# Loading heads in sets of four of one side, through GpSimd's queue, with direct moves on SyncE's

## The chip, the cores and the metric

One core of one Trainium2 chip. The time is device microseconds of one launch; a comparison goes by the median of several runs. The kernel is written by hand in a language in which the order of the instructions of each engine is the order in which the program records them, and in which every engine works through its own queue in order: TensorE (PE), VectorE (DVE), ScalarE (ACT), GpSimd (POOL) and SyncE (SP), which only issues DMAs.

## The reference

Batch 4, 8 heads, 768 tokens, 64 dimensions of a head; all tensors are fp32.

```python
q_bits = (einsum('bhsd,dk->bhsk', q, proj) > 0)      # 6 bits, the same for k
mask   = q_bucket[..., :, None] == k_bucket[..., None, :]
scores = where(mask, q @ k.T / 8, -1e9)
attn   = softmax(scores) ;  attn_out = attn @ v
x      = attn_out as (4*768 tokens, 8*64)
h      = maximum(x @ w1, x @ w2, x @ w3)             # 512 -> 768
out    = h @ w_out                                   # 768 -> 512
```

A query sees only the keys whose six signs of a projection are its own.

## The kernel before, in words

**S, the operand of the scores.** For every head the scores need q and k with the head dimension on the partitions, and below it rows of +0.5 or -0.5, the hash bits (six, padded to eight). So one matmul over 64 + 8 = 72 rows gives the dot product and, added to it, a number that is largest where all bits agree; one exp with a bias then gives nearly zero for every other key. The tile S holds 72 rows, four slots of 768 columns in bf16. Before, a tile S belongs to a *pair*: two q heads and the same two k heads of one batch.

**How a pair is prepared**, in this order: `load` (L97) brings the pair's k and q into `nat` from HBM, two DMAs of 384 KB on SyncE. `turn` (L133) transposes 32 x 32 blocks on VectorE, four instructions T<-nat of 128 x 384, written at a step of four elements. `narrow` (L137) scales T to bf16 on GpSimd. `place` (L142, L147) writes that to DRAM (`td`) and reads it back in another order into rows 0 to 63 of S: three DMAs on SyncE. `hashes` (L153, L157, L160) projects T by fp32 matmuls (bp), VectorE takes the signs (`bits`), a DMA writes them to DRAM (`bd`); two units later `place_bits` (L164) reads them into rows 64 to 71 of S, again on SyncE. The scores of the pair wait for all of this. Pair 0 alone takes a shorter way: TensorE transposes it (L291), ACT and VectorE write S from PSUM.

**Units and groups.** A unit is one head, one half of the queries (384) and two blocks of 128 keys: two score matmuls (L179) and one exp on ACT (L181). Six units are a group (two heads, half the queries), eight groups a batch; there are 192 units. The order is batch, half, pair, so the first four groups touch all four pairs of batch 0. After a group come the `values` (av, L192) and `sums` (sm, L206) matmuls of its units, in a burst: every two units for units under 24, then every six, from unit 48 on every twelve. `normalize` gathers the sums by a DMA (dd, L233), inverts them on VectorE, spreads them over the partitions by way of DRAM (rd, rb, L240, L244) and scales the values into xT (L249), steps that are due 0, 5, 7, 11 and 12 units after the burst.

**FFN.** The tokens of one half of one batch make one FFN: 18 groups of four matmuls (L265) whose maximum VectorE keeps (ht, L269 and L271), then three output blocks (L278, copied by ACT in L281, sent by SyncE). These are put between units by a credit: each unit earns 0.68, a first-layer group costs 0.66, an output block 1.32. The first FFN starts at unit 37.

**What sets the order.** The main loop goes unit by unit: scores of the next unit, then whatever was put down for this unit by `when(u, ...)` or is due in `steps`, then FFN groups, then a burst. All DMAs but the weights' and the projection's go through SyncE's queue in this order, and a DMA there that waits for its data holds up those behind it. Weights come through GpSimd's queue at units 10 to 24. PSUM has two tiles for scores, one for av and three ("ms") for everything else.

Of the kernel before, what the change touches and what calls it, by code (L numbers as in the profile page):

```python
# [9 lines left out]
FP32 = mybir.dt.float32  # L10
# [7 lines left out]
def kernel(  # L18
# [30 lines left out]
    NU_G = NM  # L49
# [12 lines left out]
    nat_pool = ctx.enter_context(tc.tile_pool(name="nat", bufs=3))  # L62
    t32_pool = ctx.enter_context(tc.tile_pool(name="t32", bufs=2))
    t16_pool = ctx.enter_context(tc.tile_pool(name="t16", bufs=2))
    s_pool = ctx.enter_context(tc.tile_pool(name="spool", bufs=7))
    b_pool = ctx.enter_context(tc.tile_pool(name="bpool", bufs=2))
    vn_pool = ctx.enter_context(tc.tile_pool(name="vnpool", bufs=3))
    vo_pool = ctx.enter_context(tc.tile_pool(name="vopool", bufs=7))
# [5 lines left out]
    h_pool = ctx.enter_context(tc.tile_pool(name="hpool", bufs=10))  # L74
# [8 lines left out]
    pst = konst.tile([P, 2, NBITS], FP32, name="pst")  # L83
    ones = konst.tile([P, Q], FP16, name="ones")
    at_tiles = [konst.tile([P, 2, HALF + 2], FP16, name=f"AT{i}", tag=f"AT{i}") for i in range(NAT)]
# [3 lines left out]
    nat, t32, t16, s_of, vnat, vo = {}, {}, {}, {}, {}, {}  # L89

    def load(pi):
        b, jj = divmod(pi, HPAIR)
        nat[pi] = nat_pool.tile([P, NC * D], FP32, tag="nat", name="nat")
        for side, src in ((1, k), (0, q)):
            nc.sync.dma_start(nat[pi][side * D : (side + 1) * D, :],  # L97
                              src[b, 2 * jj : 2 * jj + 2].rearrange("h (t c) d -> (h t) (c d)", c=NC))

    def load_by_m(pi, m0, m1):  # L100
        b, jj = divmod(pi, HPAIR)
        if pi not in nat:
            nat[pi] = nat_pool.tile([P, NC * D], FP32, tag="nat", name="nat")
        n4 = nat[pi].rearrange("p (cc m d) -> p cc m d", cc=CC, d=D)
        for side, src, eng in ((1, k, nc.sync), (0, q, nc.scalar)):
            s4 = src[b, 2 * jj : 2 * jj + 2].rearrange("h (t cc m) d -> (h t) cc m d", cc=CC, m=NM)
            eng.dma_start(n4[side * D : (side + 1) * D, :, m0:m1, :], s4[:, :, m0:m1, :])

    def load_v(pi):
        b, jj = divmod(pi, HPAIR)  # L110
        vnat[pi] = vn_pool.tile([P, 2, NM * D], FP32, tag="vnat", name="vnat")
        nc.sync.dma_start(vnat[pi][:], v[b, 2 * jj : 2 * jj + 2].rearrange("h (p m) d -> p h (m d)", p=P))

    def cast_v(pi):
        vo[pi] = vo_pool.tile([P, 2, NM * D], FP16, tag="vo", name="vo")
        nc.gpsimd.tensor_copy(vo[pi][:], vnat.pop(pi)[:])  # L116
# [11 lines left out]
    def turn(pi, u, m0, m1):  # L128
        if pi not in t32:
            t32[pi] = t32_pool.tile([P, 2, S], FP32, tag="T32", name="T32")  # L130
        i_ = nat[pi].rearrange("p (cc m u d) -> p u m cc d", cc=CC, u=2, d=Q)[:, u, m0:m1]
        o = t32[pi].rearrange("p u (m t cc) -> p u m cc t", t=Q, cc=CC)[:, u, m0:m1]
        nc.vector.transpose(o, i_)  # L133

    def narrow(pi):
        t16[pi] = t16_pool.tile([P, 2, S], BF16, tag="T16", name="T16")
        nc.gpsimd.tensor_scalar(out=t16[pi][:], in0=t32[pi][:], scalar1=RS, scalar2=1.0,  # L137
                                op0=AluOp.mult, op1=AluOp.mult)

    def place(pi):  # L140
        td = drp.tile([P, 2, S], BF16, tag="td", name="td")
        nc.sync.dma_start(td[:], t16.pop(pi)[:])  # L142
        s = s_pool.tile([KR, 4, S], BF16, tag="S", name="S")
        s_of[pi] = s
        tv = td.rearrange("(x d) u n -> u d x n", d=Q)
        for u in range(2):
            nc.sync.dma_start(s[u * Q : (u + 1) * Q, :, :], tv[u])  # L147

    def hashes(pi):
        bp = ms_ps.tile([P, 512], FP32, tag="ms", name="bp")  # L150
        for u in range(2):
            for j in range(NJ):
                nc.tensor.matmul(bp[Q * j : Q * (j + 1), 0:JW], pj[:, u, :], t32[pi][:, u, j * JW : (j + 1) * JW],  # L153
                                 start=(u == 0), stop=(u == 1))
        del t32[pi]
        bits = b_pool.tile([P, JW], BF16, tag="bits", name="bits")
        nc.vector.tensor_scalar(out=bits[:], in0=bp[:, 0:JW], scalar1=0.0, scalar2=0.5,  # L157
                                op0=AluOp.is_gt, op1=AluOp.subtract)
        bd = drp.tile([KB, 4 * S], BF16, tag="bd", name="bd")
        nc.sync.dma_start(bd.rearrange("b (x j n) -> j (b x) n", x=4, j=NJ), bits[:])  # L160
        return bd

    def place_bits(pi, bd):
        nc.sync.dma_start(s_of[pi][D:KR].rearrange("b x n -> b (x n)"), bd[:])  # L164


    units = [(b, qh, jj, kp, hd) for b in range(B) for qh in range(2) for jj in range(HPAIR)
             for kp in range(MH) for hd in range(2)]
    NU = len(units)
    UPB = NU // B  # L170
    xts, avs_of, ys_of, sm_of, av_of = {}, {}, {}, {}, {}

    def scores(u):
        b, qh, jj, kp, hd = units[u]
        s = s_of[b * HPAIR + jj]
        sc = sc_ps.tile([P, 2, 512], FP32, tag="sc", name="sc")
        for j in range(2):
            m = 2 * kp + j
            nc.tensor.matmul(sc[:, j, 0:HALF], s[0:KR, 2 + hd, m * P : (m + 1) * P],  # L179
                             s[0:KR, hd, qh * HALF : (qh + 1) * HALF], start=True, stop=True)  # L180
        nc.scalar.activation(at_tiles[u % NAT][:, :, 0:HALF], sc[:, :, 0:HALF], ActFn.Exp, bias=EXP_BIAS, scale=SCALE)  # L181

    def values(g, kps):
        b, qh, jj = units[g * NU_G][0:3]
        if kps[0] == 0:
            av_of[g] = av_ps.tile([P, 512], FP32, tag="av", name="av")
        for kp in kps:
            for j in range(2):
                m = 2 * kp + j
                for hd in range(2):  # L190
                    at = at_tiles[(g * NU_G + 2 * kp + hd) % NAT]
                    nc.tensor.matmul(av_of[g][hd * D : (hd + 1) * D, 0 : HALF + 1],  # L192
                                     vo[b * HPAIR + jj][:, hd, m * D : (m + 1) * D], at[:, j, 0 : HALF + 1],
                                     start=(m == 0), stop=(m == NM - 1))

    def sums(g, kps):
        if kps[0] == 0 and g % 2 == 0:
            sm_of[g // 2] = ms_ps.tile([P, 512], FP32, tag="ms", name="sm")
        sm = sm_of[g // 2]
        for kp in kps:  # L200
            for j in range(2):
                m = 2 * kp + j
                for hd in range(2):
                    r = 2 * hd + g % 2
                    at = at_tiles[(g * NU_G + 2 * kp + hd) % NAT]
# [3 lines left out]
    def take_av(g):  # L209
        avs_of[g] = avs_pool.tile([P, HALF + 4], FP32, tag="avs", name="avs")  # L210
        nc.vector.tensor_copy(avs_of[g][:, 0 : HALF + 1], av_of.pop(g)[:, 0 : HALF + 1])  # L211

    def take_sums(gp):
        ys_of[gp] = ys_pool.tile([P, HALF], FP32, tag="ys", name="ys")
        nc.vector.tensor_copy(ys_of[gp][:], sm_of.pop(gp)[:, 0:HALF])


    def normalize(gp):
        h, jp = divmod(gp, 2)
        if jp == 0:  # L220
            xts[h] = x_pool.tile([P, NJC, HALF], FP16, tag="xT", name="xT")
        xt = xts[h]
        W = 4 * HALF // P
        ys = ys_of.pop(gp)
        avs = [avs_of.pop(2 * gp + i) for i in range(2)]
        dd = small.tile([P, W], FP32, tag="dd", name="dd")
        rr = small.tile([P, W], FP32, tag="rr", name="rr")
        sv = small.tile([P, 2], FP32, tag="sv", name="sv")
        rd = drp.tile([4, HALF], FP32, tag="rd", name="rd")
        rb = rb_pool.tile([P, 2, HALF], FP32, tag="rb", name="rb")  # L230

        def gather():
            nc.sync.dma_start(dd[:], ys[0 : P : Q, :])  # L233
            for i in range(2):
                nc.gpsimd.tensor_scalar_mul(sv[:, i : i + 1], avs[i][:, HALF : HALF + 1], EPS)  # L235

        def invert():
            nc.vector.tensor_scalar(out=rr[:], in0=dd[:], scalar1=EPS * S, scalar2=None, op0=AluOp.add)  # L238
            nc.vector.reciprocal(rr[:], rr[:])
            nc.sync.dma_start(rd.rearrange("r (p i) -> (r p) i", i=W), rr[:])  # L240

        def spread():
            for hd in range(2):
                nc.sync.dma_start(rb[hd * D : (hd + 1) * D].rearrange("p g i -> p (g i)"),  # L244
                                  rd[2 * hd : 2 * hd + 2, :].rearrange("(o g) i -> o (g i)", o=1)
                                  .to_broadcast((D, 2 * HALF)))

        def scale(i):
            return lambda: nc.vector.scalar_tensor_tensor(  # L249
                out=xt[:, 2 * jp + i, :], in0=avs[i][:, 0:HALF], scalar=sv[:, i : i + 1], in1=rb[:, i, :],  # L250
                op0=AluOp.add, op1=AluOp.mult)

        return [(0, gather), (5, invert), (7, spread), (11, scale(0)), (12, scale(1))]


    def ffn_groups(h):
# [16 lines left out]
        rows = out[b * S : (b + 1) * S, :].rearrange("(p m) f -> p m f", m=NM)  # L273
        for tb in range(MH):
            def go2(tb=tb):
# [6 lines left out]
                nc.sync.dma_start(rows[:, qh * MH + tb, :], osb[:])  # L282
            gs.append((1.32, go2))
        return gs


    def first_turn(i):
        mp = ms_ps.tile([P, 512], FP32, tag="ms", name="mp")
        for cc in range(CC):
            c = NM * cc + 2 * i  # L290
            nc.tensor.transpose(mp[:, cc * P : (cc + 1) * P], nat[0][:, c * D : (c + 2) * D], iden[:])  # L291
        return mp

    def first_evac(i, mp, e):
        o = s_of[0][0:D].rearrange("d x (m t cc) -> d m x t cc", m=NM, cc=CC)
        i_ = mp.rearrange("p (cc x t) -> p x t cc", cc=CC, x=4)
# [198 lines left out]
```

## Time and profile before

| | us |
|---|---|
| runs shown (3): median | 357.13 (356.72 to 358.3) |
| the profiled execution | 353.46 |
| its span | 351.7 |
| TensorE busy, share of the span | 295.4 (84%) |
| VectorE busy | 183.9 (52%) |
| ACT busy | 166.4 (47%) |
| GpSimd busy | 51.8 (15%) |
| mean granted TensorE clock | 0.921 |
| bytes moved by DMA | 48.45 MB, 138 GB/s |

The profile is one execution. The span runs from its first to its last instruction; the profiled execution's own time is a little longer, by what lies around it. A share of busy time is a mean over stages with different bounds, so the profile is read here by stages, and the clock is read beside it: TensorE's granted clock is a share of full speed, and at 0.50 a matmul takes twice as long. A row of the timeline gives the start, the busy time, the engine, the line, the operation, how often it stands there, and in brackets how long the engine was idle before it and what ended that. "SPq" is SyncE's queue: its rows are the issues of DMAs, not the transfers.

### The profile page before, as it was taken

To read this page: it belongs to the slowest core of one execution; us is meant where nothing else is said; L and a number is where in the kernel's file an instruction comes from. 1 tells how busy PE (TensorE), PEld (TensorE's weight loads), DVE (VectorE), ACT (ScalarE), POOL (GpSimd) and SP (SyncE) were. 2 spreads that over 40 slices of the span, in tenths; PEclk is the share of its full clock that TensorE was granted. 3 is DMA by queue.
4 is the path that set the end of the run, shared out by engine and by line. 5 is a ranking of instruction groups with operands and counts; after the bars stand their busy time and mean duration, and the time that the engine had idled before them with its cause. 6 is when DMAs were issued, how large, how long until landed. Compare 5 with 4: busy or idle time off the path is not lost.

```text
span 351.7 us, 5705 instructions
## 1 busy us (share of the span) xinstructions
PE 295.4 (84%) x2156; PEld 151.4 (43%) x2156; DVE 183.9 (52%) x369; ACT 166.4 (47%) x221; POOL 51.8 (15%) x81
## 2 busy tenths in 40 slices
PE   2660568798998969899989998999899999999495
PEld 1120221223554545454545454545454554555162
DVE  1790221153578355863585558645843662565281
ACT  3050144364454836466646574657366648461001
POOL 3021045001223020101121201011220000000000
PEclk9997585556899999999999999999999999999899
DMA  8708389966668574629575736295343103010302
GB/s 187 171 25 216 130 193 204 166 154 170 214 162 204 174 197 135 179 61 247 171 177 151 219 109 179 70 252 156 137 119 120 30 18 105 32 48 25 111 2 89
DMA packets 31095, 48.45 MB, mean 138 GB/s; under 512 B 9188, under 2 KB 21988, under 8 KB 31068
## 3 DMA queue, kind: packets, MB, share of 16 engines
q1 hardware_dynamic: 26428, 44.54, 45.8%
q0 software_dynamic: 4096, 3.15, 5.9%
q10 hardware_dynamic: 544, 0.39, 0.5%
q8 instruction: 17, 0.28, 0.3%
q14 instruction: 10, 0.08, 0.1%
HBM read 38.10 MB, written 13.03 MB: 145 GB/s over the span
## 4 chain that ended last, share of the span: by engine, by line
PE 57%; DMA 17%; DVE 9%; ACT 7%; issue 5%; SPq 3%; POOL 1%; ACTq 0%; DVEq 0%; POOLq 0%
PE l L265 21%; PE sc L179 11%; PE av L192 10%; PE sm L206 6%; ACT AT L181 5%; DVE T L133 5%; DMA bd<-bits 4%; DMA dd<-ys 4%; PE l L278 4%; PE bp L153 3%; DMA S<-bd 2%; DMA rb<-rd 2%; DMA pst<-in_proj_dram 2%; DMA td<-T 2%; ACT osb L281 2%
## 5 line engine op out<-in xcount | busy, mean ns | idle before, releaser
L181 ACT ACTIVATE AT<-sc 128x768 f16<-128x768 f32 x192 | 151.3, 812 | 143.5 <-PE sc L179 143.3
L265 PE MATMUL l<-xT,w_sb 128*128 128x384 f16 x576 | 112.9, 328 | 12.0 <-DVE ht L271 6.2
L179 PE MATMUL sc<-S 72*128 72x384 bf16 x384 | 96.4, 350 | 27.7 <-DMA S<-bd 20.8
L265 PEld LDWEIGHTS <-w_sb 128*128 128x128 f16 x576 | 56.0, 97 | 53.9 <-issue 17.3
L179 PEld LDWEIGHTS <-S 72*128 72x128 bf16 x384 | 36.6, 102 | 68.3 <-issue 27.8
L271 DVE TENSOR_TENSOR ht<-ht,l 128x384 f16<-128x384 f16 x96 | 53.0, 552 | 22.4 <-PE l L265 18.5
L133 DVE STREAM_TRANSPOSE T<-nat 128x384 f32<-128x384 f32 x64 | 47.8, 844 | 8.2 <-DMA nat<-in_q_dram 8.2
L192 PE MATMUL av<-AT,vo 128*64 128x385 f16 x384 | 43.8, 359 | 1.9 <-DVE avs L211 1.9
L249 DVE SCALAR_TENSOR_TENSOR xT<-avs,sv,rb 128x384 f16<-128x384 f32 x32 | 19.0, 617 | 44.1 <-DMA rb<-rd 44.0
L137 POOL TENSOR_SCALAR T<-T 128x1536 bf16<-128x1536 f32 x15 | 22.0, 1470 | 121.0 <-issue 84.7
L278 PE MATMUL l<-wout_sb,ht 128*128 128x512 f16 x144 | 34.4, 379 | 0.0
L206 PE MATMUL sm<-AT,ones 128*32 128x384 f16 x384 | 32.1, 349 | 0.0
L269 DVE CAST ht<-l 128x384 f16<-128x384 f32 x48 | 26.3, 548 | 10.7 <-PE l L265 10.2
L211 DVE COPY avs<-av 128x385 f32<-128x385 f32 x32 | 17.9, 558 | 24.1 <-PE av L192 23.9
L192 PEld LDWEIGHTS <-vo 128*64 128x64 f16 x384 | 19.4, 115 | 23.9 <-issue 16.6
L281 ACT COPY osb<-l 128x512 f32<-128x512 f32 x24 | 14.1, 586 | 33.0 <-PE l L278 33.0
L235 POOL TENSOR_SCALAR sv<-avs 128x1 f32<-128x1 f32 x32 | 7.3, 229 | 127.7 <-DVE avs L211 118.2
L153 PE MATMUL bp<-T,pj 128*32 128x192 f32 x240 | 20.3, 349 | 1.2 <-DVE T L133 1.2
L278 PEld LDWEIGHTS <-ht 128*128 128x128 f16 x144 | 14.0, 97 | 15.0 <-DVE ht L271 0.2
L206 PEld LDWEIGHTS <-ones 128*32 128x32 f16 x384 | 13.1, 98 | 15.9 <-issue 12.2
L116 POOL CAST vo<-vnat 128x768 f16<-128x768 f32 x16 | 13.2, 825 | 18.4 <-DMA vnat<-in_v_dram 15.5
L238 DVE TENSOR_SCALAR rr<-dd 128x12 f32<-128x12 f32 x16 | 3.0, 186 | 23.4 <-DMA dd<-ys 23.3
(25 smaller groups left out, 60.6 us busy)
## 6 DMA issues: line engine op xcount, KB each, us to landing
vnat<-in_v_dram SPq DMA_DIRECT2D x16, 384.0 KB
rb<-rd SPq DMA_DIRECT2D x32, 192.0 KB
out_dram<-osb SPq DMA_DIRECT2D x24, 256.0 KB
nat<-in_k_dram SPq DMA_DIRECT2D x15, 384.0 KB
nat<-in_q_dram SPq DMA_DIRECT2D x15, 384.0 KB
td<-T SPq DMA_DIRECT2D x15, 384.0 KB
S<-td SPq DMA_DIRECT2D x30, 192.0 KB
w_sb<-in_moe_w_dram POOLq DMA_DIRECT2D x6, 384.0 KB, 7.4
```

What stands on the lines that cost most here:

```text
L133: nc.vector.transpose(o, i_)
L137: nc.gpsimd.tensor_scalar(out=t16[pi][:], in0=t32[pi][:], scalar1=RS, scalar2=1.0, op0=AluOp.mult, op1=AluOp.mult)
L153: nc.tensor.matmul(bp[Q * j : Q * (j + 1), 0:JW], pj[:, u, :], t32[pi][:, u, j * JW : (j + 1) * JW], start=(u == 0), stop=(u == 1))
L179: nc.tensor.matmul(sc[:, j, 0:HALF], s[0:KR, 2 + hd, m * P : (m + 1) * P], s[0:KR, hd, qh * HALF : (qh + 1) * HALF], start=True, stop=True)
L181: nc.scalar.activation(at_tiles[u % NAT][:, :, 0:HALF], sc[:, :, 0:HALF], ActFn.Exp, bias=EXP_BIAS, scale=SCALE)
L192: nc.tensor.matmul(av_of[g][hd * D : (hd + 1) * D, 0 : HALF + 1], vo[b * HPAIR + jj][:, hd, m * D : (m + 1) * D], at[:, j, 0 : HALF + 1], ...
L206: nc.tensor.matmul(sm[Q * r : Q * (r + 1), 0:HALF], ones[:, :], at[:, j, 0:HALF], start=(m == 0), stop=(m == NM - 1))
L265: nc.tensor.matmul(ps[:, 0:HALF], w_sb[wi][:, jc, fb * P : (fb + 1) * P], xt[:, jc, :], start=(jc == 0), stop=(jc == NJC - 1))
L269: nc.vector.tensor_copy(hts[fb][:], ps[:, 0:HALF])
L271: nc.vector.tensor_tensor(out=hts[fb][:], in0=hts[fb][:], in1=ps[:, 0:HALF], op=AluOp.max)
L278: nc.tensor.matmul(ps[:, 0:DM], hts[fb][:, tb * P : (tb + 1) * P], wout_sb[:, fb, :], start=(fb == 0), stop=(fb == NFB - 1))
L281: nc.scalar.copy(osb[:], ps[:, 0:DM])
```

## The change

1. **Sets.** Batch 0 keeps its pairs. From batch 1 on, a tile S holds four heads of one side: four k heads or four q heads. A table `where` tells the scores in which tile and slot a head lies.
2. **Queues.** The sets' loads (one DMA of 768 KB), all of v (four DMAs for four heads) and the weights are issued by GpSimd. SyncE issues k of the pairs, and ACT q of the pairs; SyncE also keeps the small moves and the output.
3. **Placing.** `place` copies T in bf16 straight from SBUF into S, four DMAs of 32 partitions for each half of the head dimension, so eight for a set; `narrow` is done in the same two halves. `td` is gone. The bits still go by DRAM.
4. **Transposes** write without gaps; the order of the tokens in a tile is now (block, cc, t), and v and the output rows follow it.
5. **Order.** Group 1 is now the second half of pair 0, so pair 1 is first needed at unit 12, pair 2 at 18, pair 3 at 24. Bursts are every two units up to unit 30. Groups under unit 48 are normalised singly. The first two FFNs are put down at units 43 and 61, the later ones one unit later than before; a unit earns 0.69.
6. **Start.** The projection comes by one DMA, the first of GpSimd's queue. Twelve matmuls on a zeroed tile run ahead of the first real one (their result is not used). One of the last two PSUM evacuations of pair 0 goes to ACT.
7. Buffers: nat 4, t16 3, v 2 (of four heads), vo 4 (of four heads), ht 9.

The diff, cut to its core:

```diff
+    def load_pair(pi, pieces=((0, NM),)):
+        start_set(("p", pi), [(0, 2 * pi), (0, 2 * pi + 1), (1, 2 * pi), (1, 2 * pi + 1)])
...
+            for side, src, eng in ((1, k, nc.sync), (0, q, nc.scalar)):
...
+                eng.dma_start(o, i_)
+    def load_quad(side, g):
+        start_set((side, g), [(side, 4 * g + x) for x in range(4)])
+        nc.gpsimd.dma_start(nat[side, g][:], by_rows((q, k)[side], 4 * g, 4))
+    def load_v(g, n0=0, n1=4):
...
+        for cc in range(CC):
+            nc.gpsimd.dma_start(vnat[g][cc * Q : (cc + 1) * Q, n0:n1, :], src[cc])
...
-        o = t32[pi].rearrange("p u (m t cc) -> p u m cc t", t=Q, cc=CC)[:, u, m0:m1]
-        nc.vector.transpose(o, i_)
+        nc.vector.transpose(t32[name][:, u, m0 * P : m1 * P], i_)
...
-    def place(pi):
-        td = drp.tile([P, 2, S], BF16, tag="td", name="td")
-        nc.sync.dma_start(td[:], t16.pop(pi)[:])
...
-        for u in range(2):
-            nc.sync.dma_start(s[u * Q : (u + 1) * Q, :, :], tv[u])
+    def place(name, u):
...
+        for x in range(4):
+            nc.sync.dma_start(s_of[name][u * Q : (u + 1) * Q, x, :], t[x * Q : (x + 1) * Q, :])
...
+    groups[0:8] = [(0, 0, 0), (0, 1, 0), (0, 0, 1), (0, 0, 2), (0, 0, 3), (0, 1, 1), (0, 1, 2), (0, 1, 3)]
...
     with tc.manual_schedule():
-        load_by_m(0, 0, 4)
-        load_by_m(0, 4, 6)
+        nc.gpsimd.dma_start(pst[:], proj.rearrange("(u d) k -> d u k", d=Q))
+        load_pair(0, ((0, 4), (4, 6)))
+        nc.vector.memset(warm[:], 0.0)
         make_identity(nc, iden[:])
-        for x in range(4):
-            nc.gpsimd.dma_start(pst[x * Q : (x + 1) * Q], proj.rearrange("(u d) k -> d u k", d=Q))
-        load_v(0)
-        load(1)
-        load_v(1)
-        load(2)
+        load_v(0, 0, 2)
+        load_pair(1)
+        load_v(0, 2, 4)
+        load_pair(2)
+        load_v(1)
...
+        wp = ms_ps.tile([P, 512], FP32, tag="ms", name="wp")
+        for n in range(12):
+            nc.tensor.matmul(wp[:, 0:HALF], warm[:, 0:P], warm[:, :], start=True, stop=True)
...
+        def prepare(name, u_turn, u_hash):
             for n in range(4):
                 u2, mh = divmod(n, 2)
+                when(u_turn + n // 2, lambda u2=u2, mh=mh: turn(name, u2, 3 * mh, 3 * mh + 3))
+            for u2 in range(2):
+                when(u_turn + 1 + u2, lambda u2=u2: narrow(name, u2))
+                when(u_turn + 3 + u2, lambda u2=u2: place(name, u2))
+            hash_at.append((u_hash, name))
+        when(1, lambda: cast_v(0, 2, 4))
+        when(1, lambda: load_pair(3))
+        prepare(("p", 1), 0, 3)
+        prepare(("p", 2), 4, 8)
+        when(8, lambda: cast_v(1))
+        prepare(("p", 3), 8, 13)
+        uh = {(1, 2): 30, (0, 2): 36, (1, 3): 42, (0, 3): 48}
...
+            when(u2 - 16, lambda side=side, g=g: load_quad(side, g))
+            prepare((side, g), u2 - 6, u2)
...
-            when(10 + 2 * n, lambda i=i, half=half: load_weights(i, half))
+            when(6 + 3 * n, lambda i=i, half=half: load_weights(i, half))
...
+        ffn_at = {30 + 13: 0, 48 + 13: 1}
+        for h in range(2, 2 * B - 1):
+            ffn_at[24 * (h + 1) + 14] = h
```

## The prediction

> **What bounds the kernel now.** I read the windows (busy time of each engine by stage) first, then the timeline, the chain of waits and SyncE's queue.
>
> ```profile
> 20.00:30.00 10.00, 4.40 (x36) 1.25 (x32) 6.59 (x10) 2.19 (x3) 3.76 (x3) 1.00 0.28 85
> 30.00:40.00 10.00, 0.59 (x2) 0.28 (x3) 1.54 (x2) 0.00 (x0) 0.82 (x1) 0.50 0.72 202
> ...
> 60.00:70.00 10.00, 6.37 (x26) 1.78 (x27) 0.96 (x3) 3.03 (x4) 0.21 (x1) 0.50 1.13 179
> 70.00:80.00 10.00, 9.42 (x35) 2.66 (x33) 5.13 (x10) 6.28 (x9) 0.89 (x2) 0.50 0.68 164
> ...
> 100.00:120.00 20.00, 18.94 (x158) 10.55 (x157) 13.14 (x27) 10.21 (x13) 6.00 (x7) 1.00 0.63 172
> ```
>
> Columns: stage, its length, busy PE, weight loads, DVE, ACT, POOL, granted clock, DMA share, GB/s. From 100 us on PE is busy 17 to 20 us of each 20 at clock 1.00: there TensorE is the bound. Before 94 us it is not: it stands still, or runs at clock 0.50. The timeline's PE rows say for what:
>
> ```profile
> 39.41 1.46 PE L179 MATMUL sc<-S 72*128 72x384 bf16 x4 [13.80 <-DMA S<-bd]
> ...
> 51.03 1.46 PE L179 MATMUL sc<-S 72*128 72x384 bf16 x4 [3.27 <-DMA S<-bd]
> ...
> 63.63 1.44 PE L179 MATMUL sc<-S 72*128 72x384 bf16 x4 [3.73 <-DMA S<-bd]
> ...
> 93.65 2.12 PE L265 MATMUL l<-xT,w_sb 128*128 128x384 f16 x12
> ```
>
> These are units 6, 12 and 18 (one unit: two score matmuls and one exp): the first units of pairs 1, 2 and 3, each waiting for the pair's hash rows, which come last into S. Unit 37, with the first FFN matmul, comes at 93.65. So the change is worth what it does to 0 to 94 us, plus any change in the rate after. What lies before S, from SyncE's queue:
>
> ```profile
> 24.98 0.35 SPq L142 DMA_DIRECT2D td<-T  x1
> 27.32 0.81 SPq L147 DMA_DIRECT2D S<-td  x2
> 28.23 0.47 SPq L97 DMA_DIRECT2D nat<-in_k_dram  x1
> 28.76 0.59 SPq L97 DMA_DIRECT2D nat<-in_q_dram  x1
> 29.40 1.09 SPq L112 DMA_DIRECT2D vnat<-in_v_dram  x2
> 30.59 0.67 SPq L160 DMA_DIRECT2D bd<-bits  x1
> 37.20 0.31 SPq L164 DMA_DIRECT2D S<-bd  x1
> ```
>
> The bits were ready at 25.2 (row L157, 24.83 plus 0.36). SyncE got to them at 30.59, after the DRAM bounce and three bulk loads; bd then took 6.6 us and S 2.2.
>
> **Part by part.**
>
> *Start.* proj's copies came in four DMAs (issued 1.50 to 3.9, pj copied until 10.6), and the first transpose waited for the last. Now one DMA stands first on GpSimd: issued about 0.4, landing 5.0 later by the first one's row (1.50 to 6.50), four pj copies of 0.17 with gaps: transposes from 6.5, not 10.65. Score 0 came 6.6 us after that (17.2): now 13.1, unless k and q are later (PE had the first piece at 5.71). The twelve warm-up matmuls (at most 12 x 0.33 = 4 us at the half rate) end before 5.7 and I give them nothing: the trace grants 1.00 from 0 to 30 us without them.
>
> *Both halves of pair 0 first.* Pair 1 is needed at unit 12, not 6. At full clock two early units take 1.7 us (43.62 to 45.27: two exps of 0.81 bound them), so units 0 to 11 last 10.2, plus 1 for PE's wait on pair 1's transposes: unit 12 is due at 24.3.
>
> *Small moves.* td and the DRAM read go (2.3 to 4.6 us a pair by the td rows), and the bulk loads leave SyncE. In their place stand eight DMAs a pair, at 0.40 us of issue each (two S<-td: 0.81). The built program's queues add one thing: each DMA of SyncE and ACT waits for the one eight places earlier to have landed (so before, but with three DMAs a pair). That puts new waits where it matters. The last of pair 1's eight pieces waits for pair 3's q load, which ACT issues after its third exp (about 15.5). By then 4.6 MB are asked for; at the 190 to 215 GB/s of the first ten microseconds and of 30 to 40 they are in at 22 to 23. Pair 1's bd goes out behind it: 23, though its bits are ready at 20.3. For pairs 2 and 3 a late piece waits for the *previous* pair's S<-bd. So the three chains run one after another. A link is bd, then S<-bd: rows 6.6, 3.0, 5.0, 2.5 and 2.2, 3.9, 5.5, means 4.3 and 3.8, sum 8.1 (4.7 to 12.1). Between them SyncE issues 1.4 us of pieces and dd, before pair 3 with rd, rb and dd 2.5. Sum: S of pair 1 at 23 + 8.1 = 31.1; pair 2 at 31.1 + 1.4 + 8.1 = 40.6; pair 3 at 51.2. By the short rows 27.7, 33.8, 41.0; by the long ones 35.1, 48.6, 63.2. Units 12, 18 and 24 start there (before: 51.0, 63.6, 72.4).
>
> *Clock.* PE stands still from 24.3 to 31, longer than the 3.3 us after which it fell to 0.50 at 50.8. Cold, two units take 2.93 us (63.63 to 66.54), six 8.8; they fit between the S times, so the cold clock costs something only after unit 24: 24 to 29 take 8.8 (5.1 warm): unit 30 at 60.0. Units 30 to 42 run in bursts of six, whose rows (75.34 to 85.22 to 93.32) give 9.9 and 8.1, mean 9.0: 13 units, 19.5 us (14.3 if always warm: 5.0 of exps and the uncovered rest of a 3.1 us burst). Unit 43, the first with FFN, at 79.5; by the short bounds 60.4, by the long 93.4.
>
> *After that.* From unit 37 the kernel before takes 351.7 - 93.65 = 258.1. The new one enters at unit 43, so six units' matmuls are done: scores 0.33 each, values 1.11 and sums 0.72 a group, 3.8 together; one hash fewer is left (0.95); the FFN tail is 0.6 longer (6.9 instead of 7.5 credits spent on half 6). The FFN itself is only put later: it is all still there and keeps PE full to the end. 258.1 - 3.8 - 0.95 + 0.6 = 253.9. Single-group normalisations (seven more chains dd, rd, rb) fall before unit 60 and lie beside exps.
>
> *Contiguous transposes.* L133 takes 846 ns (median) for 384 fp32; DVE ops of 384 with a dense output take 548 (L269). The gain is 0 to 0.30 us each; in the ramp SyncE hides it, later about ten T rows stand on the chain, before an FFN evacuation. I take 2 us, nearer to the slow row (0 to 6). Halved narrows (0.74 each by L137), one cast for four heads, GpSimd's issues (0.79 by L122): under 4 us of GpSimd per 12 units (17.6 us), nothing, as long as DVE's transposes find their data.
>
> *Sum.* 79.5 + 253.9 - 2 = 331.4 span; before had 353.46 - 351.7 = 1.76 outside it: 333.2 against the profiled 353.46. The median of the runs shown is 3.67 above the profiled execution, so 336.8; I give **336**.
>
> **Rivals.**
>
> *SyncE's ring of eight eats the gain* (0.15): links at the long rows, because weight loads now start at unit 6 and share the engines (53 to 63 us before: DMA share 1.2 to 1.3, links of 10.4). Unit 43 at 93, span 347, about 351. For it: every link is serial. Against: GpSimd issues those weights between waiting narrows, so they come spread out.
>
> *Warm and short* (0.20): short links, PE never still for over 3 us, unit 43 at 60: span 314, about 318. For it: the link from 44.16 to 51.03 took 7 under load, the bd at 85.75 only 2.5. Against: pair 1 misses unit 12 by 3.4 us even by the short rows.
>
> *Long links, but warm* (0.05): PE comes back to 1.00 soon after each stall. Then units 24 to 29 take 5.1 and 30 to 42 14.3: 3.7 + 5.2 less, 327. Against: from 63.63 to 75 PE was dense and stayed at 0.50; it rose at 43.5 and 84.7, both times during fp32 hash matmuls. The Trainium skill would have it so (TensorE: Matmul & The Clock Gate, Part 1: some 3.4 us of sustained matmuls bring the full rate back); by those 11 us the trace does not agree.
>
> *Slower: late bulk loads hold DVE* (0.07). Every T from unit 24 on waits for a load issued ten units earlier through GpSimd, 14.7 us at the steady 1.47 us a unit. DVE works in order: behind a waiting T stand the FFN evacuations, and PE, with three "ms" banks, stops within 2 us. GpSimd-issued loads of 768 KB of source (w) landed in 7.4 us, wout in 11.2. If one takes over 14.7, each of the twelve sets costs the excess; from 1.8 us of excess on (16.5 of landing) the 21 us gained are gone, at 17.5 it is 2.8 x 12 = 34 less 21, 13 slower than before: about 370. Against: a margin of 3.5 us over the slowest row. The Trainium skill (SBUF — State Buffer, SBUF: two separate sides) says that DVE operations which take both of its SBUF port pairs keep GpSimd from writing descriptors; by it such loads starve while DVE is busy, and this rival comes nearer. The weights issued by GpSimd at 47 to 59 went out while DVE was nearly idle, so the trace shows neither.
>
> *It does nothing* (0.03): no single stall is removed, only moved; 357. Each S time above would have to be missed by 20 us.
>
> The rest, 0.50, is the forecast (325 to 346). The range takes in most of its neighbours: **316 to 351**. 0.5% is about what a measurement of this kernel can tell from no change; faster by more: 0.88 (forecast, short, warm, and most of the ring), same 0.04, slower 0.08.
>
> **What would show it.** Right: first score near 13; PE waiting for S<-bd before units 12, 18, 24 at about 31, 41, 51; SyncE waiting for DMAs on its pieces; first FFN matmul near 80; from there the same 1.46 us a unit. Wrong: S<-bd links under 5 us; clock 1.00 between 31 and 60; DVE T rows waiting for nat after 100 us; T at 550 ns and a clearly faster steady part, which would put the end below the forecast.

## The result, and the profile after

The changed kernel takes 383.44 us (median of four runs, 379.59 to 388.34); the kernel before 356.93 (four runs). The ratio of comparable runs is 1.0645, 95% interval 1.0556 to 1.0734: **slower**, where 336 was forecast. Two of the four runs, at 387 and 388 us, were disturbed and are not in the ratio. The profiled execution is 379.92 us, its span 378.1, its mean granted clock 0.86 (before: 353.46, 351.7, 0.921).

The windows of after, most of them the stages shown of before (same columns: length, PE, weight loads, DVE, ACT, POOL, clock, DMA share, GB/s):

```profile
20.00:30.00 10.00, 10.00 (x63) 3.50 (x64) 3.79 (x8) 4.54 (x6) 5.83 (x7) 0.50 0.62 116
30.00:40.00 10.00, 8.53 (x70) 3.19 (x64) 3.54 (x8) 4.82 (x7) 4.55 (x7) 0.85 0.75 118
60.00:70.00 10.00, 7.00 (x29) 1.95 (x29) 5.54 (x14) 3.71 (x5) 5.22 (x9) 0.50 0.55 114
...
100.00:120.00 20.00, 20.00 (x139) 11.12 (x138) 13.14 (x30) 12.99 (x16) 4.22 (x6) 0.97 0.40 104
...
240.00:260.00 20.00, 13.73 (x91) 7.47 (x85) 8.71 (x19) 7.20 (x9) 5.28 (x9) 0.87 0.40 106
```

From 30 to 40 PE now works where it stood still. But it runs cold from 20 to 30, is no better off from 60 to 70, and, which nobody expected, idles a third of the time from 240 to 260, in the part that was PE-bound. The timeline's PE rows of after, in answer to the three stalls shown of before:

```profile
40.82 0.95 PE L192 MATMUL sc<-S 72*128 72x384 bf16 x4
...
52.05 0.85 PE L206 MATMUL av<-AT,vo 128*64 128x385 f16 x4 [8.59 <-DVE avs L210]
...
56.53 1.46 PE L192 MATMUL sc<-S 72*128 72x384 bf16 x4
...
63.92 0.85 PE L206 MATMUL av<-AT,vo 128*64 128x385 f16 x4 [3.00 <-DVE avs L210]
...
68.39 1.46 PE L192 MATMUL sc<-S 72*128 72x384 bf16 x4
...
91.47 0.65 PE L272 MATMUL l<-xT,w_sb 128*128 128x384 f16 x3
93.28 0.32 PE L272 MATMUL l<-xT,w_sb 128*128 128x384 f16 x1 [1.16 <-DVE xT L256]
97.20 2.72 PE L272 MATMUL l<-xT,w_sb 128*128 128x384 f16 x8 [3.60 <-DVE bits L171]
```

The score rows at 40.82, 56.53 and 68.39 are units 18, 24 and 30. The waits for S<-bd are gone. In their place PE waits for VectorE's copy of `av`, and the first FFN matmul, of unit 43, comes at 91.47; at 79.5 it was forecast. From it to the end are 378.1 - 91.47 = 286.6 us, against a forecast of 253.9 less 2. So about 12 us are lost before unit 43 and 35 after it. From 100 us to the end PE is not busy for 37 us, before for 22, and its mean clock there is 0.92, before 0.99: in the windows in which it stands still longest (140 to 160, 180 to 200 and 240 to 260) the clock is 0.83 to 0.87. What VectorE's scaling of the values waits for, by the waits in total (us, times, longest); first after:

```profile
DVE xT L256 <- DMA rb<-rd: 87.3, 18, 10.9
```

and before:

```profile
DVE xT L249 <- DMA rb<-rd: 44.0, 12, 7.8
```

The chain of waits gives DMA 29% of the span, before 17%. What holds rb late in the steady part shows in SyncE's queue of after:

```profile
125.83 0.57 SPq L237 DMA_DIRECT2D dd<-ys  x1
127.11 0.56 SPq L289 DMA_DIRECT2D out_dram<-osb  x1
129.99 0.55 SPq L289 DMA_DIRECT2D out_dram<-osb  x1
130.63 0.44 SPq L244 DMA_DIRECT2D rd<-rr  x1
137.49 1.18 SPq L248 DMA_DIRECT2D rb<-rd  x2
```

rb is issued when rd (6 KB) has landed: 6.9 us after rd's issue here. In the kernel before, with rd issued at 122.86, it was 1.8. Ahead of this rd stand two output blocks, whose DMAs have a new shape; the next rd, at 152.95 with none just ahead of it, took 1.6. The DMA view of the last 18 us, where the three last output blocks go out alone, first after (360 to 378 in 40 slices, share of 16 engines in tenths, and what they moved):

```profile
DMA  0000000000000000430032222222222222221000
GB/s 0 0 0 0 0 0 0 0 0 0 0 0 0 0 0 5 50 14 5 32 64 77 100 96 105 100 105 100 100 109 100 100 100 100 109 96 64 18 0 0
```

then before (340 to 351.7):

```profile
DMA  0000002000000000000000069603990089500000
GB/s 0 0 0 0 0 0 56 0 0 0 0 0 0 0 0 0 0 0 0 0 0 0 0 259 385 252 0 126 371 378 21 0 343 371 182 0 0 0 0 0
```

Before, a block of 256 KB was out in about 0.9 us (three slices) at up to 385 GB/s with nearly all engines. After, it moves at 100 GB/s with a share of 0.2, about four engines of sixteen, for some 2.5 us each, one behind the other: from the issue of the first of these three (366.01) to the end are 12.1 us, before 5.7. The block is now written as 4 x 32 x 512 (`rows "(t cc m) f -> m cc t f"`) and no longer as 128 x 512. The Trainium skill (DMA: Bandwidth & Descriptors, "Why a DMA increments its semaphore by 16 and not by 1") has the rule: a DMA runs on the largest k up to 16 that divides the slowest dimension, longer than 1, of both access patterns. For 4 and 128 that is 4; the share of 0.2 agrees.

### The profile page after: what moved, and what is told of

Read it like the earlier page. It is cut to its first block, busy times and chain, and to the rows that moved or that the text cites. A ratio compares the mean times of both kernels' runs of the same rounds, so it can differ in the third digit from the quotient of the medians.

```text
span 378.1 us, 5980 instructions
## 1 busy us (share of the span) xinstructions
PE 315.1 (83%) x2168; PEld 157.3 (42%) x2168; DVE 169.1 (45%) x381; ACT 167.8 (44%) x222; POOL 78.2 (21%) x134
## 4 chain that ended last, share of the span: by engine, by line
PE 51%; DMA 29%; SPq 7%; DVE 7%; issue 2%; ACT 1%; POOL 0%; DVEq 0%; ACTq 0%
PE l L272 20%; PE sc L192 11%; DMA dd<-ys 9%; DMA rd<-rr 9%; PE av L206 8%; DMA rb<-rd 7%; PE l L285 6%; SPq L160 4%; PE sm L219 4%; PE bp L168 3%; DMA nat<-in_k_dram 3%; SPq L248 2%; DVE T L148 2%; DMA S<-T 1%; DVE xT L256 1%
## 5 line engine op out<-in xcount | busy, mean ns | idle before, releaser
L272 PE MATMUL l<-xT,w_sb 128*128 128x384 f16 x576 | 121.6, 343 | 18.9 <-DVE xT L256 7.7
L192 PE MATMUL sc<-S 72*128 72x384 bf16 x384 | 100.4, 361 | 3.6 <-ACT AT L194 3.5
L272 PEld LDWEIGHTS <-w_sb 128*128 128x128 f16 x576 | 58.4, 101 | 65.2 <-issue 30.9
L206 PE MATMUL av<-AT,vo 128*64 128x385 f16 x384 | 47.6, 381 | 18.6 <-DVE avs L210 18.6
L256 DVE SCALAR_TENSOR_TENSOR xT<-avs,sv,rb 128x384 f16<-128x384 f32 x32 | 19.2, 616 | 87.3 <-DMA rb<-rd 87.3
L152 POOL TENSOR_SCALAR T<-T 128x768 bf16<-128x768 f32 x30 | 24.9, 831 | 90.1 <-DVE T L148 37.1
L206 PEld LDWEIGHTS <-vo 128*64 128x64 f16 x384 | 21.0, 120 | 42.4 <-issue 35.8
L219 PE MATMUL sm<-AT,ones 128*32 128x384 f16 x384 | 34.1, 359 | 0.0
L148 DVE STREAM_TRANSPOSE T<-nat 128x384 f32<-128x384 f32 x64 | 32.5, 547 | 3.4 <-DMA nat<-in_k_dram 3.3
L125 POOL DMA_DIRECT2D vnat<-in_v_dram x36 | 20.0, 561 | 7.8 <-DMA vnat<-in_v_dram 7.5
L168 PEld LDWEIGHTS bp<-T,pj 128*32 128x32 f32 x240 | 11.6, 132 | 12.4 <-DVE ht L278 7.9
```

The costliest lines, as they stand in the source:

```text
L148: nc.vector.transpose(t32[name][:, u, m0 * P : m1 * P], i_)
L152: nc.gpsimd.tensor_scalar(out=t16[name, u][:], in0=t32[name][:, u, :], scalar1=RS, scalar2=1.0, op0=AluOp.mult, op1=AluOp.mult)
L192: nc.tensor.matmul(sc[:, j, 0:HALF], s_of[kn][0:KR, kx, m * P : (m + 1) * P], s_of[qn][0:KR, qx, qh * HALF : (qh + 1) * HALF], start=True, ...
L219: nc.tensor.matmul(sm[Q * r : Q * (r + 1), 0:HALF], ones[:, :], at[:, j, 0:HALF], start=(m == 0), stop=(m == NM - 1))
L256: nc.vector.scalar_tensor_tensor(out=xts[h][:, jj, :], in0=avs[i][:, 0:HALF], scalar=sv[:, i : i + 1], in1=rb[:, i, :], op0=AluOp.add, op1 ...
L272: nc.tensor.matmul(ps[:, 0:HALF], w_sb[wi][:, jc, fb * P : (fb + 1) * P], xt[:, jc, :], start=(jc == 0), stop=(jc == NJC - 1))
```

## The experiments

Each ratio is against the kernel before on the same chip.

**e1: the output block in four DMAs.** After, with

```diff
-                nc.sync.dma_start(rows[qh * MH + tb], osb[:])
+                for cc in range(CC):
+                    nc.sync.dma_start(rows[qh * MH + tb, cc], osb[cc * Q : (cc + 1) * Q, :])
```

> The new kernel, with each output block sent by four DMAs of 32 rows instead of one DMA whose output side is 4 x 32 x 512. Theory A (the output DMAs run on few engines, hold the small DMAs behind and beside them, and so VectorE and TensorE): outputs no longer sit at a DMA share of 0.2 and 100 GB/s for 7 us; the wait of VectorE for rb falls from 87 us to 50 or less; the part after the first FFN matmul falls from 287 us to 255 to 265; about 350 us. Theory B (GpSimd's bulk loads crowd the small DMAs): nothing changes but the tail, 375 to 383 us. Theory C (the loss lies in the first 92 us, in the singly normalised groups and the half clock): part after 92 us unchanged, 378 to 383 us.

Measured: 358.7 us, ratio 0.9959 (0.9908 to 1.001), span 354.6. One line of the change gives back 24.5 us (1.0645 less 0.9959, of 356.93). From the first FFN matmul on it takes 264.0 us, as Theory A said. VectorE's wait for rb did not fall to 50: it is 77.2 in total, 36.9 of it in the first 100 us (35.7 of 87.3 in after). From 100 us on, PE's time without work falls from 37 to 22 us and its clock rises from 0.92 to 0.97.

**e2: the new output map alone, in the kernel before.** Its output rows land in another order.

```diff
-        rows = out[b * S : (b + 1) * S, :].rearrange("(p m) f -> p m f", m=NM)
+        rows = out[b * S : (b + 1) * S, :].rearrange("(t cc m) f -> m cc t f", cc=CC, m=NM)
```

> The kernel before, with its output blocks sent by the new kernel's row map, so by one DMA of 4 x 32 x 512 (the rows of the output land in another order). Theory A: slower by much of what the new kernel loses after its first FFN matmul, 370 to 390 us, with waits of VectorE for rb well above 44 us. Theory B and C: 357 us, at most 3 to 5 us more at the tail.

Measured: 389.58 us, ratio 1.0888 (1.0814 to 1.0962), span 387.8. Nothing else differs from before, and VectorE's wait goes from 44.0 to

```profile
DVE xT L249 <- DMA rb<-rd: 73.0, 13, 11.0
```

The last three blocks again move at 100 to 105 GB/s with a share of 0.2. Done alone and undone alone, the map is shown to be the cause of the loss.

**e3: the bulk loads of sets and v back on SyncE.**

```diff
-        nc.gpsimd.dma_start(nat[side, g][:], by_rows((q, k)[side], 4 * g, 4))
+        nc.sync.dma_start(nat[side, g][:], by_rows((q, k)[side], 4 * g, 4))
...
-            nc.gpsimd.dma_start(vnat[g][cc * Q : (cc + 1) * Q, n0:n1, :], src[cc])
+            nc.sync.dma_start(vnat[g][cc * Q : (cc + 1) * Q, n0:n1, :], src[cc])
```

> The new kernel, with the loads of sets and of v issued by SyncE instead of GpSimd. Theory B: rb lands sooner, the wait of VectorE for rb falls to about 50 us, 355 to 365 us. Theory A: the output DMAs are as before, after the first FFN matmul still about 285 us, 375 to 395 us.

Measured: 385.58 us, ratio 1.0734 (1.0634 to 1.0835); VectorE waits 95.3 us for rb. No gain: which queue issues the loads is not the cause, and my rival of late loads falls with it.

**e4: no warm-up matmuls** (the twelve matmuls on `wp` left out).

> The new kernel without the twelve warm-up matmuls. If the warm-up is worth something, the first transposes and hashes run at half rate (first score at 15 instead of 13.9 us). If it also shifts the moment at which the clock falls, units 0 to 11 may run at 1.00 as they did before the change: then unit 12 comes at 26 instead of 33.6, and the time falls by up to 8 us. If the warm-up is worth nothing, 378 to 385 us.

Measured: 382.75 us, ratio 1.0697 (1.0617 to 1.0778), not to be told from after. Yet the warm-up does something. The first PE rows of after, and below them those of e4:

```profile
5.69 1.08 PE L300 MATMUL mp<-iden,nat 128*128 128x128 f32 x8 [0.56 <-DMA nat<-in_k_dram]
7.46 1.48 PE L319 MATMUL bp<-T,pj 128*8 128x384 f32 x16 [0.69 <-DVE T L148]
11.15 0.63 PE L300 MATMUL mp<-iden,nat 128*128 128x128 f32 x4 [2.20 <-DMA nat<-in_k_dram]
```

```profile
5.88 1.94 PE L300 MATMUL mp<-iden,nat 128*128 128x128 f32 x8 [5.88 <-DMA nat<-in_k_dram]
7.75 2.75 PE L319 MATMUL bp<-T,pj 128*8 128x384 f32 x16
11.17 0.63 PE L300 MATMUL mp<-iden,nat 128*128 128x128 f32 x4 [0.67 <-DMA nat<-in_k_dram]
```

Without it the first transposes and hashes take 1.8 to 1.9 times as long; but both kernels then wait for the second piece of nat, at 11.15, so nothing of it reaches the first score.

**e6: the token order taken at the loads, not at the output.** With e1 the loss is gone, but the forecast gain is still missing. Here q, k and v come in an order in which an output block is one DMA of 128 rows again, as before, on all engines. The pairs after the first take their q loads on SyncE too. The transposes stay contiguous.

```diff
+    def head(src, hh, name, x, eng, m0=0, m1=NM):
+        i_ = src[hh // H, hh % H].rearrange("(cc t m) d -> t cc (m d)", cc=CC, m=NM)[:, :, m0 * D : m1 * D]
+        o = nat[name][x * Q : (x + 1) * Q, :].rearrange("p (cc c) -> p cc c", cc=CC)[:, :, m0 * D : m1 * D]
+        eng.dma_start(o, i_)
...
-        nc.gpsimd.dma_start(nat[side, g][:], by_rows((q, k)[side], 4 * g, 4))
+        for x in range(4):
+            head((q, k)[side], 4 * g + x, (side, g), x, nc.gpsimd)
...
-        for cc in range(CC):
-            nc.gpsimd.dma_start(vnat[g][cc * Q : (cc + 1) * Q, n0:n1, :], src[cc])
+        nc.gpsimd.dma_start(vnat[g][:, n0:n1, :], v[b, h0 + n0 : h0 + n1].rearrange("h (p m) d -> p h (m d)", p=P))
...
-        rows = out[b * S : (b + 1) * S, :].rearrange("(t cc m) f -> m cc t f", cc=CC, m=NM)
+        rows = out[b * S : (b + 1) * S, :].rearrange("(p m) f -> p m f", m=NM)
```

> The new kernel with another order of the tokens, taken at the loads: each partition gets four runs of 1536 B, one DMA of 32 partitions a head, v again comes as one DMA and an output block is one DMA of 128 rows, with the transposes still contiguous. Theory A: outputs on all engines with a quarter of e1's issues, so as fast as e1 or some us faster, 350 to 357 us. Rival: four loads a set through GpSimd and shorter runs cost what the outputs gain, 357 to 365 us.

Measured: 343.96 us, ratio **0.96** (0.9492 to 0.9709), span 338.4: faster than both kernels. Its last blocks move at up to 396 GB/s, its first FFN matmul comes at 90.3, and from there the rest takes 248.1. In e1 it takes 354.6 - 90.55 = 264.0, of which 8.5 go at once: PE's first FFN there stops at 90.55 and runs on at 99.08 (waits of 5.42 for xT, 1.98 for `bits`). e6 also saves three of four issues a block (one block issues in 0.3 to 0.6 us, four pieces in 1.7 to 3.0), and moves a block faster than four pieces together (their tail runs at 90 to 174 GB/s). How the 16 us split between these, and what the other loads give, I did not measure.

**e5, e7: single-group normalisations later** (their steps 3 and 6 units later, the first two FFNs 6 units later), in e1 and in e6.

```diff
-        return [(0, gather), (5, invert), (7, spread)] + [(11 + i, lambda i=i: scale(i)) for i in range(n)]
+        late = 3 if n == 1 else 0
+        return [(0, gather), (5 + late, invert), (7 + late, spread)] + [(11 + 2 * late + i, lambda i=i: scale(i)) for i in range(n)]
...
-        ffn_at = {30 + 13: 0, 48 + 13: 1}
+        ffn_at = {30 + 19: 0, 48 + 19: 1}
```

> Output in four DMAs as in the run e1, and the singly normalised groups (units under 48) take their inversion 3 units later and their scaling 6 units later; the first two FFNs are put down at units 49 and 67 for it. Theory C (in the first 99 us VectorE, in order, stands at the scaling of a single group, whose rb has not landed, and the copy that frees TensorE's only av bank stands behind it): the waits of TensorE for that copy (7.7 and 3.1 us) go, unit 43 comes at 78 to 84 instead of 90.6, and the time falls by 8 to 15 us, to about 345. Rival: the DMA engines are full there anyway (share 1.2 at 40 to 50 us), the wait moves to another instruction, within 3 us of e1.

> e6 and e5's later single groups together. If both hold, the gains add: 338 to 347 us, faster than the kernel before by 3 to 5%. If the first 99 us are bound by the DMA engines, as e6.

Measured: e5 362.34 us, ratio 1.0169 (1.0071 to 1.0268); e7 345.34, ratio 0.9723 (0.9653 to 0.9792). e5 misses. e7's time lies in its range, but e6's does too, and e7's ratio is no better. PE's waits for `avs` shrink to 1.1 us at most, but it stops ahead of a score instead: in e5 6.1 us at 35.2 and 4.0 at 48.6 (e1: 2.9 at 33.0), in e7 4.8 at 30.6, as in e6, and 7.1 at 56.8. The first FFN, now at unit 49, comes at 102.3 and 95.8. Unit 43's scores come 1.8 and 2.8 us earlier than in e1 and e6 (85.1 for 87.0, 82.4 for 85.2), which the six units put in front of the FFN take back. Most of the wait was moved, not removed.

**e8: weights ten units later** (e1, with `when(16 + 3 * n, ...)` for `when(6 + 3 * n, ...)`).

> e1 with the weight loads put down at units 16 to 37 instead of 6 to 27. Theory D (it is the weight loads that make rd, dd and rb land late in 38 to 62 us: rd took 6.1, dd 7.9): these fall to 2 to 4 us, VectorE's wait for rb falls by 10 us or more, and the time by 5 to 12. Theory C alone: the waits stay within 3 us in sum, 352 to 357 us.

Measured: 359.07 us (355.23 to 363.54, kernel before 354.58), span 355.7 against e1's 354.6: no gain. The first FFN comes at 93.6, in e1 at 90.55, and VectorE waits 82.1 us for rb, in e1 77.2: Theory D falls.

**e9, e10, e11: the clock, and VectorE's order, in e6's first 90 us.** e9 puts a full-array matmul on zeros ahead of each score matmul of units 0 to 47; e10 gives the scaling of the single groups to GpSimd; e11 does both.

```diff
+            if u < 48:
+                nc.tensor.matmul(sc[:, j, 0:HALF], warm[:, 0:P], warm[:, :], start=True, stop=True)
             nc.tensor.matmul(sc[:, j, 0:HALF], s_of[kn]...
```

> The kernel of e6 with one more matmul ahead of each score matmul of units 0 to 47 (96 of 128x128x384 on a tile of zeros, into the bank that the score then overwrites). Theory C (the first 43 units are late because TensorE runs them at half clock; in e6 its granted clock is 0.50 from 50 to 70 us although PE is busy in 54 to 58 and 66 to 70 without a gap): the full-array matmuls lift the clock to 1.00 in those stretches, and the first FFN matmul comes before 87 (e6: 90.3), 340 us or less. Theory L (they are late because the small moves S, dd, rd and rb take 4 to 6 us each beside the bulk loads; the clock only follows the waits): the fillers fill waiting time at most, the waits for S and avs stay where they were, first FFN at 90 to 96 and 344 to 350 us. If the clock stays at 0.50 under the fillers too, 96 x 0.33 = 32 us more PE work is put in front of the FFN: up to 365.

> The kernel of e6 with the final scaling of the five single-group normalisations done by GpSimd in two instructions (add, multiply) in place of VectorE's one. Theory V (VectorE waits in order for rb, 10.0 and 7.4 us in e6, and so copies avs late, for which PE waits 6.9 and 3.0 us): both PE waits go, first FFN 3 to 10 us earlier, 334 to 341 us. Rival: GpSimd waits in its place, and the casts of T and the bulk loads behind it are late: S of the later pairs late by the same 5 to 10 us, no gain, 343 to 352.

> e9 and e10 together. Theories C and V both true: 330 to 337. C alone or V alone: near the better of the two. Theory L: as e9, 344 to 352, since S and rb land when they land.

Measured: e9 344.37 us, ratio 0.9626 (0.9569 to 0.9682); e10 342.2, 0.9555 (0.9482 to 0.9627); e11 341.84, 0.9566 (0.9521 to 0.9612). None is to be told from e6 (0.96). The clock did rise. Windows of e6:

```profile
14.00:30.00 16.00, 11.95 (x90) 4.25 (x88) 7.53 (x16) 7.06 (x10) 7.41 (x9) 0.80 0.81 156
30.00:46.00 16.00, 12.25 (x68) 4.19 (x69) 1.61 (x5) 7.57 (x10) 5.69 (x10) 0.68 1.07 191
46.00:62.00 16.00, 8.87 (x36) 2.37 (x36) 3.53 (x10) 4.54 (x6) 4.00 (x7) 0.55 0.76 143
```

and of e9:

```profile
14.00:30.00 16.00, 13.24 (x107) 5.30 (x105) 7.44 (x16) 7.22 (x10) 7.46 (x9) 1.00 0.75 154
30.00:46.00 16.00, 12.76 (x87) 5.47 (x88) 2.22 (x5) 7.67 (x10) 5.60 (x9) 0.89 0.89 158
46.00:62.00 16.00, 9.03 (x47) 3.26 (x47) 2.40 (x6) 3.25 (x5) 3.99 (x7) 0.68 0.83 163
```

0.55 to 0.80 became 0.68 to 1.00, but ACT did no more work in the three together (18.1 us of exps, 19.2 in e6), and the first FFN came at 91.5. Theory C falls as it was put: a higher clock did not bring the FFN earlier. But the clock rose only in part, and the fillers take PE time themselves, so what a higher clock alone would give is not shown here. In e10 PE still waits 5.79 and 5.04 us for `avs`, for VectorE now stands longer at the next instruction in its order, the inversion that waits for dd (59.3 us in total, 14.9 in e6): the gain that Theory V forecast does not come, though VectorE's order is still what PE waits for.

**e12, e13: without the bulk of the weights.** e12 is e6 with the eight weight loads replaced by GpSimd filling zeros (the output is zero); e13 adds e9's matmuls.

> The kernel of e6 with the eight FFN weight loads (6.3 MB of source between 20 and 90 us, of some 15 MB in all) left out: GpSimd fills the weights with zeros at the same places, so the output is zero and only the time counts. Theory B2 (dd, rd, rb and the S moves take 4 to 6 us each in the ramp because the bulk loads keep the DMA engines full, share 0.8 to 1.3 up to 80 us in e6): the waits for avs (6.9 and 3.0 us) shrink by over half, first FFN before 84 (e6: 90.3), 336 us or less. Theory Q (they are late by their order in SyncE's queue, each waiting for the one before, whatever else moves; e8, with the weights only put later, was no different): first FFN at 87 to 91, 339 to 346 us.

> e12 and e9 together: no weight loads (output zero), and the 96 full-array matmuls that held the granted clock near 1.00 in e9. Theory W (two limits, each of which covers the other: with the clock up the units wait for the small moves, with shorter moves they run at 0.50): first FFN below 80 (e9 91.5, e12 85.1) and 331 us or less. Rival (the moves in SyncE's order are the only limit, and the 5 us of e12 were all there is): first FFN at 84 to 87, 335 to 338 us.

Measured: e12 336.2 us, ratio 0.9362 (0.9271 to 0.9452), first FFN 85.1; e13 337.31, ratio 0.9374 (0.9296 to 0.9452), first FFN 83.7. e12 lies between its two theories: the loads are worth 5 us of the first FFN, not more. e13 refutes Theory W. Its PE is warm (0.89 to 1.00 from 14 to 78), yet its first FFN stops after three matmuls and goes on at 90.06: PE's longest wait, 5.8 us, is for xT, and VectorE's rows say why:

```profile
45.99 0.62 DVE L257 SCALAR_TENSOR_TENSOR xT<-avs,sv,rb 128x384 f16<-128x384 f32 x1 [8.93 <-DMA rb<-rd]
54.92 0.62 DVE L257 SCALAR_TENSOR_TENSOR xT<-avs,sv,rb 128x384 f16<-128x384 f32 x1 [7.12 <-DMA rb<-rd]
...
89.39 0.62 DVE L257 SCALAR_TENSOR_TENSOR xT<-avs,sv,rb 128x384 f16<-128x384 f32 x1 [8.96 <-DMA rb<-rd]
```

The first group's dd is issued at 30.46, rr started at 32.91, rd issued at 39.23, rb at 42.58, xT made at 45.99: 15.5 us, of which 6.3 lie between rr and rd, while SyncE issues the next pair's bits and pieces ahead of it (bd at 33.70, S<-bd at 36.12). By these rows the chain and its place in the order are what is left. No run here took it out of the way, so that it sets the stretch is argued, not shown.

## Why the prediction was wrong

**The step that failed is one that was not there.** Under *Contiguous transposes* I priced T's new layout, and took the rest of that edit (v and the output rows that follow the new token order) at nothing, without a row. The output's DMAs had a row for the old shape only; the new one, 4 x 32 x 512, takes four engines. It cost 24.5 us undone (e1) and 31.7 done alone (e2: 0.0888 of 356.93). So *After that*, 253.9 less 2 from the first FFN matmul on, was 286.6. By the same measure, without the map, the step was near: e6 takes 248.1, 3.8 under it; e1 takes 264.0, 12.1 over it, of which 8.5 are the stop of its first FFN.

**Unit 43 at 79.5** came at 91.47, and at 90.3 in e6: 11 to 12 us too early in the forecast. Up to unit 18 the run was on time (40.82, forecast 40.6). Unit 24 came at 56.53 (51.2), unit 30 at 68.39 (60.0), and the first FFN matmul 23.1 us later (19.5). Three sub-steps failed, and the first of them cost little.

*Both halves of pair 0 first*, PE through with units 0 to 11 at 24.3. It was through at 33.6, since its clock fell to 0.50 at 12.6. I read clock 1.00 from 0 to 30 in the trace of before; but its first hash matmuls took 2.75 us, as e4's cold ones do, so PE was cold under that figure:

```profile
11.56 2.75 PE L310 MATMUL bp<-T,pj 128*8 128x384 f32 x16 [3.92 <-DVE T L133]
```

The forecast let unit 12 wait for pair 1 until 31.1 anyway. In e1 and e4 the clock was back at 1.00 before 25 us; PE was through with unit 11 at about 30 and then stood 2.94 and 4.47 us, until 32.98 and 34.32, hardly another time than 33.60. In e9, warm until 30, it stood until 30.92. The row of e1 (the bracket names the semaphore that came last by the profile; S<-bd had been issued at 28.72):

```profile
32.98 0.81 PE L192 MATMUL sc<-S 72*128 72x384 bf16 x4 [2.94 <-DMA dd<-ys]
```

*Single-group normalisations lie beside exps*, cost nothing. This lost most. VectorE works in order: while it waits for the first group's rb, the copy of the next `av` stands behind it, and PE waits 8.59 us between units 18 and 24, and 3.00 behind the next group between 24 and 30:

```profile
50.64 0.62 DVE L256 SCALAR_TENSOR_TENSOR xT<-avs,sv,rb 128x384 f16<-128x384 f32 x1 [10.95 <-DMA rb<-rd]
```

I said this of a waiting T row in the slower rival, and did not ask it of xT. With the clock lifted in part the waits were there still (8.42 and 3.40 in e9). But behind them stands another: in e7, without them, PE stood 7.14 us for pair 3 and unit 24 came at 56.77, for its S<-bd was issued at 52.86 (e6: 49.76). What unit 43 would gain if both went is not shown.

*Clock*, units 30 to 42 in 19.5 us. The first FFN matmul stands behind the scores of unit 44, so these are fourteen units and not thirteen; they took 22.7.

**Start** came near: score 0 at 13.87, forecast 13.1, though the last wait was for the second piece of nat (11.15), not for the projection. **Warm-up: nothing** was right in the sum (e4), for a wrong reason: PE was cold without it, and the second piece of nat hides what it saves.

**Small moves** hit the times, in part by luck. bd of pairs 1, 2 and 3 was issued at 25.93, 34.50 and 48.53, where the forecast had 23, 32.5 and 43.1; S<-bd followed 2.4 to 2.8 us later, where bd was put at 4.3. No PE wait ends on S<-bd in after; where PE stood ahead of unit 12 in other runs, the scores followed its issue by 2.2 (e12) to 4.4 us (e10). By an estimate with these two, pair 1 was ready at 30.5 to 32.7, pair 2 at 39.5 to 40.8, where its scores begin, and pair 3 at 53.2 to 55.4; forecast 31.1, 40.6 and 51.2. Later starts and shorter links cancel. PE came to each pair at most about 3 us after it was ready, so the links did not hold PE in after, but they were close behind, as e1, e4 and e7 show.

**Contiguous transposes**: 547 ns a row where 846 stood, the full 0.30; 64 rows, 15 us of VectorE less.

**Clock**, that PE stays at 0.50 through dense work, held in after: from 20 to 30 us PE is busy 10.00 of 10 at 0.50. It is no rule: in e1 and e4, which run the same instructions there, the clock in that window is 0.77 and 0.78, back at 1.00 after some 7 us at 0.50. The Trainium skill's rule (TensorE: Matmul & The Clock Gate, Part 1: some 3.4 us of sustained matmuls restore the full rate) does not fit those ten us of after; e1 and e4 took about twice its figure. With full-array matmuls among the scores (e9) the clock stays at 1.00 from 14 to 30.

**The slower rival** had the right sign and the wrong mechanism: VectorE waited for nat once, 3.3 us at the start, and e3, with the loads on SyncE, was no better. Without the map, what was forecast at 336 of 357.13 (ratio 0.941) measures 0.996 with e1's repair and 0.960 with e6's, which also changes the loads. The 7 us missing in e6 (0.019 of 357.13) are unit 43's 10.8, less the 3.8 by which the part after it was better.

**Open:** how the 16 us between e1 and e6 split; what brings the clock back after 7 us in e1 and e4 and not after ten in after; and whether another order of the single-group chains would bring unit 43 to 80. Giving them more units (e5, e7) did not.

## What to carry to other kernels

When a layout is changed at one end, follow it to every DMA that must undo it, and count the outer dimension of each new access pattern: a shape of 4 x 32 rows used about a quarter of the DMA engines here. The last blocks themselves paid 6.4 us for it (12.1 against 5.7); most of the 24.5 was paid earlier, where other work waited. Take the permutation where a transfer has time (e6's loads), not where a queue is shared with a chain that others wait for. And a wait that is put on an engine which works in order costs what stands behind it, whatever lies beside it. When it is taken away, look for the next wait close behind.

## What the runs showed of the hardware

- A 256 KB write ran at about 100 GB/s as one DMA of 4 x 32 x 512 (after, e2), at 90 to 174 as four DMAs of 32 x 512 (e1), and at up to 385 (before) and 396 (e6) as one of 128 x 512.
- A 6 KB DMA issued 0.6 us behind a block of the first kind took 6.9 us until the DMA that needs it could be issued (after, 130.63); 0.5 us behind the four pieces it took 1.5 (e1, 133.15), and 1.3 us behind a block of the last kind 1.4 (e6, 129.77).
- The profile's clock reads 1.00 from the start until its first change, whatever PE does: the first eight transposes took 1.94 us under that figure without warm-up (before, e4), 1.08 with it (after).
- PE's clock stayed at 0.50 through ten dense microseconds in after (20 to 30) and came back after some 7 in e1 and e4, with the same matmuls (scores of 72 rows, values of 64 columns, hashes). With one 128 x 128 matmul to each score it stayed at 1.00 from 14 to 30 (e9).
